# Attention with memory and a bilinear GLU on one core: transfers, roundings and transposed columns set in other places between the matmuls

## The chip, the cores and the metric

One core of a Trainium2 chip runs the whole kernel. The metric is the device time of one execution in microseconds (us), the median of several runs. In the profile the engines are PE (TensorE, matmuls), PEld (its weight loads), DVE (VectorE), ACT (ScalarE), POOL (GpSimd) and SP (SyncE, which mostly issues DMAs).

## What is computed

The input x has 2048 rows of 512. A small vector c gives six modulation vectors (sa, ca, ga, sb, cb, gb). Then, with LN the layernorm of a row:

```python
h = LN(x) * (1 + ca) + sa
x = x + ga * attention(h)        # wq, wk, wv, wo, beta
h = LN(x) * (1 + cb) + sb
x = x + gb * ((h @ w_gate) * (h @ w_up)) @ w_down
```

The attention has 32 heads of 16 columns and goes through 4 segments of 512 rows. In each segment and head it takes a causal softmax, `softmax(q k^T / 4 + mask) v`, and adds to it, with a gate per head, a part from a memory M, z that holds what earlier segments have left (`phi(q) M / (phi(q) z)`). The output of all heads goes through wo. w_gate and w_up have 1376 columns.

## The kernel before

**Numbers.** Where a matmul needs fp32 exactness, each operand is split in a rounded half (H, written by ScalarE as a copy to a rounded format) and a remainder (L, the difference, on VectorE or GpSimd), and three matmuls are done: H with H, H with L, L with H. This is what "roundings" are. Keys and queries are split in three bf16 parts, and laid in DRAM (`kd`, `qd`), from which `load(u)` (L265) brings them as `kst` and `qst`, 384 KB each, for the four heads of a unit.

**Stages.** A prologue makes the modulation vectors, segment 0's layernorm and its first keys, queries and values. Then a loop over v from -2 to 32 handles 32 units u (4 segments x 4 groups of 8 heads x 2 halves) in five slots each. In a slot:

- `q_step`: scores of queries against keys on PE, two banks `q..._0` and `q..._1`, and VectorE's row maxima of them (CUSTOM_DVE q<-q,cmask with READ_ACCUMULATOR nm). The maxima of the unit end in `nm`, which is split and transposed (`n_split`, `n_step`) and written by ScalarE's DMA queue into two rows of qst.
- `k_step`: the transposed scores `k` on PE, one bank; ScalarE's exponential `pt` (L329), GpSimd's causal masking (L332).
- `av_step`: probabilities times values (`tb`), one unit later.
- `t_step`, `r_step`, `o_step`: normalise. The result goes to DRAM (`td`) and back as `rd` and `orow` rows; the reciprocals go to DRAM (`rdd`) and back broadcast as `rb`; VectorE multiplies `orow` by `rb`; the memory's part is added by GpSimd; the row goes to DRAM as `od`. For the last two groups (`last`, ug 14 and 15) PE transposes instead, VectorE divides, and the memory's part is added at L393.

**Filler work.** Between these, `fill(share)` runs pieces of two generators, `fill_a` and `fill_b`, a piece costing as much credit as it yields (0.68 for three matmuls of 512 columns, 0.0 for work off PE). `weave(a, b, at)` puts pieces of b behind those pieces of a whose numbers stand in `at`, counting only pieces that cost credit. So the tables of numbers in these two functions set where each instruction stands in every engine's queue, and each engine works its queue in order.

- `fill_a`: keys, queries and values of the next groups (`a_kq`: 12 matmuls into `kps` or `qps`, from `hH` and `hL`, the split columns of the layernorm), the memory's updates, the next segment's layernorm. Its rows are loaded by `xload` (L580); `ln_rows` takes their statistics on VectorE (BATCH_NORM_STATS2, `ast`) and normalises them; `ln_col` transposes a column block on PE (`atp`), and ScalarE scales it; ScalarE and GpSimd split it (L222, L223).
- `fill_b`: the output projections of segments 0 to 2. `wo_load` (L467) loads `orl` from `od`; `wo_op` (L475) rounds them, `oH` on ScalarE (L497), remainder into `orl` on VectorE; `wo_mm` has four rows of 12 matmuls (`wops`), after each of which VectorE adds to `xr` (`wo_add`) and a DMA writes `x1d` (L535). `lnC` (L542) reads `x1d` back (L548), takes statistics (`cst`), normalises, transposes the columns (`ctp`), scales them (`chf`, L205) and splits them (`chH`, L222): the inputs of the GLU.

After the loop comes the GLU, matmuls `g`, `up` and `acc` closely packed, with no loop work beside them.

**Queues.** SP issues nearly all DMAs in program order; an issue that waits for its data holds up all behind it.

## Time and profile before

| | |
|---|---|
| time, median of 3 runs | 868.21 us (867.92 to 868.63) |
| profiled execution: time | 872.37 us |
| profiled execution: span | 870.6 us |
| mean granted clock of PE | 0.988 |
| PE busy in the span | 833.0 us, 96% |
| DMA, mean rate over the span | 160 GB/s |

A row of a timeline gives start and duration (us), engine, line, operation, output and inputs, and in brackets the idle time ahead of it with what ended it. "x2" is two of them in one row. A row of the list of waits gives the total, the number of times and the longest, all of idle time over a threshold. In the windows, PEclk is the share of full clock that was granted.

### The profile page before, as it was taken

What the parts mean: (1) busy time and instruction counts of PE and PEld (TensorE: products, weight loads), DVE (VectorE), ACT (ScalarE), POOL (GpSimd) and SP (SyncE); (2) the same over time, 40 slices, a digit from 0 to 9 for tenths busy, and PEclk for the clock granted to TensorE, in tenths of its full rate; (3) what the DMA queues carried; (4) which work ended last, traced back from release to release, by engine and by line L of the source; (5) the groups of instructions that cost most, each with busy time, mean ns of one, the idle gap of its engine ahead of it and who ended that gap; (6) DMA issues with size and microseconds to landing.
All of it is one profiled execution on the core that took longest, in us unless ns stands there. A gap on an engine that the chain in (4) does not pass through costs nothing.

```text
span 870.6 us, 14346 instructions
## 1 busy us (share of the span) xinstructions
PE 833.0 (96%) x4824; PEld 584.8 (67%) x4824; DVE 652.7 (75%) x1728; ACT 473.9 (54%) x740; POOL 426.0 (49%) x564
## 2 busy tenths in 40 slices
PE   8999999999999999989988899999999999999998
PEld 5765566566665566655645577788778888887886
DVE  8688677888789777789878769888685666767532
ACT  3747867598667875677445664433354423333321
POOL 4435744487445754496323825998101755650000
PEclk8999999999999999999999999999999999999999
DMA  7773747468566665876794552654305231112033
GB/s 225 224 236 104 220 164 215 147 213 270 181 179 209 220 189 171 247 233 213 234 294 144 171 168 97 181 159 136 108 30 165 70 120 54 50 55 94 0 119 98
DMA packets 111355, 139.45 MB, mean 160 GB/s; under 512 B 18800, under 2 KB 70000, under 8 KB 111280
## 3 DMA queue, kind: packets, MB, share of 16 engines
q1 hardware_dynamic: 106016, 130.91, 49.0%
q10 hardware_dynamic: 5264, 7.62, 2.4%
q8 instruction: 38, 0.62, 0.3%
q14 instruction: 37, 0.30, 0.1%
HBM read 87.48 MB, written 50.76 MB: 159 GB/s over the span
## 4 chain that ended last, share of the span: by engine, by line
PE 70%; DVE 11%; DMA 7%; ACT 7%; issue 2%; POOL 2%; SPq 1%; ACTq 0%; DVEq 0%; POOLq 0%
PE g L90 23%; PE acc L90 14%; PE tb L90 6%; PE k L90 6%; PE q L90 6%; PE vps L90 4%; DVE q L40 4%; PE kps L90 3%; PE qps L90 3%; ACT pt L329 2%; DMA x1d<-xr 2%; PE wops L90 2%; PE up L90 1%; PE mz L90 1%; DVE ast L40 1%
## 5 line engine op out<-in xcount | busy, mean ns | idle before, releaser
L40 DVE CUSTOM_DVE_ANT_0 q<-q,cmask 128x384 f32<-128x384 f32 (+3 forms) x512 | 246.7, 508 | 64.6 <-PE q L90 54.6
L329 ACT ACTIVATE pt<-k 128x1024 f32<-128x1024 f32 x160 | 164.1, 1025 | 65.5 <-PE k L90 51.9
L332 POOL TENSOR_SCALAR_AFFINE_SELECT pt<-pt 128x256 f32<-128x256 f32 (+1 forms) x224 | 107.0, 491 | 148.7 <-ACT pt L329 145.8
L90 PE MATMUL q<-kst,qst 96*128 96x384 bf16 (+3 forms) x512 | 101.5, 302 | 12.1 <-DVE nm L40 9.5
L90 PE MATMUL k<-qst,kst 98*128 98x384 bf16 (+3 forms) x512 | 97.5, 303 | 8.5 <-ACT pt L329 8.4
L448 POOL TENSOR_TENSOR w<-w 128x256 f32<-128x256 f32 (+1 forms) x84 | 72.3, 873 | 57.4 <-DVE t L1216 37.9
L443 POOL TENSOR_TENSOR AL<-w,AH 128x512 fp32r<-128x512 f32 (+1 forms) x42 | 58.8, 1404 | 46.4 <-ACT AH L439 46.3
L90 PE MATMUL tb<-pt,v 128*32 128x512 f32 (+3 forms) x1024 | 78.9, 450 | 1.5 <-POOL pt L332 1.5
L90 PEld LDWEIGHTS <-kst 98*128 98x128 bf16 x512 | 38.5, 99 | 53.9 <-issue 47.5
L40 DVE DVE_READ_ACCUMULATOR2_ANT nm<- 128x1 f32 x512 | 72.4, 141 | 0.0
L439 ACT ACTIVATE AH<-w 128x512 fp32r<-128x512 f32 (+3 forms) x88 | 47.3, 565 | 43.2 <-POOL w L448 29.9
L90 PEld LDWEIGHTS <-qst 96*128 96x128 bf16 x512 | 43.5, 98 | 40.3 <-issue 13.8
L1473 DVE TENSOR_TENSOR mL<-mid,mH 128x512 fp32r<-128x512 f32 (+1 forms) x44 | 32.3, 739 | 41.5 <-ACT mH L1472 41.5
L90 PEld LDWEIGHTS tb<-pt,v 128*32 128x32 f32 x1024 | 29.6, 112 | 41.8 <-issue 36.7
L90 PE MATMUL acc<-DH,mL 128*128 128x512 f32 x144 | 56.6, 393 | 0.9 <-DVE mL L1473 0.9
L90 PE MATMUL acc<-DH,mH 128*128 128x512 f32 x144 | 57.2, 397 | 0.0
L90 PE MATMUL acc<-DL,mH 128*128 128x512 f32 x144 | 56.5, 393 | 0.0
L1472 ACT ACTIVATE mH<-mid 128x512 fp32r<-128x512 f32 (+1 forms) x44 | 27.1, 627 | 51.7 <-PE acc L90 50.4
L1265 ACT ACTIVATE p<-g 128x512 f32<-128x512 f32 (+1 forms) x22 | 13.2, 598 | 74.0 <-PE g L90 73.9
L443 DVE TENSOR_TENSOR AL<-w,AH 128x512 fp32r<-128x512 f32 (+3 forms) x44 | 32.6, 742 | 13.8 <-ACT AH L439 13.6
L358 ACT ACTIVATE tsb<-tb 128x512 f32<-128x512 f32 x32 | 19.1, 597 | 35.2 <-PE tb L90 35.1
L90 PE MATMUL g<-t_0H,AH 128*128 128x512 f32 (+1 forms) x88 | 34.9, 396 | 0.7 <-DVE u L1271 0.3
(286 smaller groups left out, 2067.3 us busy)
## 6 DMA issues: line engine op xcount, KB each, us to landing
kst<-kd SPq DMA_DIRECT2D x32, 384.0 KB
qst<-qd SPq DMA_DIRECT2D x32, 384.0 KB
td<-tsb ACTq DMA_DIRECT2D x28, 256.0 KB
wm<-in_w_mod_dram SPq DMA_DIRECT2D x24, 256.0 KB
kd<-k SPq DMA_DIRECT2D x16, 384.0 KB
qd<-q SPq DMA_DIRECT2D x16, 384.0 KB
w<-in_w_gate_dram SPq DMA_DIRECT2D x20, 256.0 KB
w<-in_w_up_dram SPq DMA_DIRECT2D x40, 128.0 KB
```

The costliest lines, as they stand in the source:

```text
L40: i = getattr(self.eng, name)(*a, **k)
L90: return pe(nc.tensor.matmul(*a, **k))
L329: lpt[0] = act.activation(pt, kp, AF.Exp, scale=0.25)
L332: sels[u, i] = nc.gpsimd.affine_select(w, w, pattern=[[0, w.shape[1]], [1, P]], compare_op=ALU.is_ge, fill=0.0, base=0, channel_multiplier=-1)
L358: act.activation(tsbs[u], tbs.pop(u), AF.Copy)
L439: i = act.activation(hi[sl], w[sl], AF.Copy)
L443: i = eng.tensor_sub(lo[sl], w[sl], hi[sl].bitcast(F32))
L448: i = ce.tensor_tensor(w[:, o, :, 0:n], w[:, x, :, 0:n], w[:, y, :, 0:n], op=op)
L1265: lcp[0] = act.activation(r["p1"], ps, AF.Copy)
L1472: pin(act.activation(mH[0:n], md[0:n], AF.Copy))
L1473: vec.tensor_sub(mL[0:n], md[0:n], mH[0:n].bitcast(F32))
```

## The change

Six things move; the number of matmuls stays.

1. **First rows.** The four rows of segment 1 were loaded two and two: two ahead of the loop's first qst loads, two later behind group 3's weights. Now all four are loaded together, behind the key loads of unit 2 and ahead of group 3's weights. The table STEPS0, which places the steps of their layernorm, follows.
2. **First keys.** For the first group of keys of segments 1 to 3 the matmuls with `hL` are put last.
3. **Last rows' sum.** The addition of L393 goes from GpSimd to VectorE.
4. **Third output's roundings and first output's columns.** `wo_op(2)` and `lnC(0)`'s columns were run one behind the other, after segment 1's output projection; now both are woven between the matmuls of the output projections of segments 1 and 2. `weave` takes several generators for it, and `lnC` has no mark (`yield False`) after each second column any more.
5. **Second output's loads and roundings.** The first two `orl` loads of segment 1 now stand ahead of xr's load, and the roundings begin one piece later.
6. `wo_load` takes the groups to be loaded.

```diff
@@ -226,8 +226,6 @@
             if kept_h is not None:
                 kept_h.append(h)
             yield 0.45
-            if pfx == "c" and d % 2 == 1:
-                yield False
         return hH, hL
 
     def run(gen):
@@ -390,7 +388,7 @@
             vec.reciprocal(rd, tr[:, :, :, DH])
             vec.tensor_mul(orow[:, :, h0:h0 + 4, :], tr[:, :, :, 0:DH], rd.unsqueeze(3).to_broadcast([P, 4, 4, DH]))
             if jq == 1:
-                nc.gpsimd.tensor_add(orows[ug], orows[ug], mems.pop(ug))
+                vec.tensor_add(orows[ug], orows[ug], mems.pop(ug))
             return
         if jq == 0:
             rds[ug] = ap.tile([P, 2, DH], F32, tag="rd", name=f"rd{ug}", bufs=1)
@@ -464,9 +462,9 @@
         wt[i] = hi, lo
         yield 0.0
 
-    def wo_load(s, pool):
+    def wo_load(s, pool, gs=range(NG)):
         rw = []
-        for g in range(NG - 2 if s == NSEG - 1 else NG):
+        for g in gs:
             a = pool.tile([P, L], F32, tag="orl", name=f"orl{s}_{g}", bufs=4)
             pin(nc.sync.dma_start(a, od[s][g]))
             rw.append(a)
@@ -674,16 +672,17 @@
     def a_ln(s):
         return ln(pa, pa, xts.pop(s), s, ca_c, sa_c, "a", ("h", 8, 3), s == 0)
 
-    def weave(a, b, at):
+    def weave(a, *bs):
 
         i = 0
         for w in a:
             yield w
             if w:
-                for _ in range(at.count(i)):
-                    w = next(b, None)
-                    if w or w is False:
-                        yield w
+                for b, at in zip(bs[::2], bs[1::2]):
+                    for _ in range(at.count(i)):
+                        w = next(b, None)
+                        if w or w is False:
+                            yield w
                 i += 1
 
     wH, wL = {}, {}
@@ -763,13 +762,13 @@
         if True:
             dst = kd if nm == "k" else qd
             ps = bank(f"{nm}ps{s}_{g}")
-            n = 0
-            for k in range(KT):
-                for a, b in ((wH, hH), (wL, hH), (wH, hL)):
-                    MM(ps, a[nm, g][:, k, :], b[k], start=n == 0, stop=n == 11)
-                    n += 1
-                    if n in (3, 6, 9):
-                        yield 0.68
+            terms = [(k, a, b) for k in range(KT) for a, b in ((wH, hH), (wL, hH), (wH, hL))]
+            if s > 0 and g == 0 and nm == "k":
+                terms.sort(key=lambda t: t[2] is hL)
+            for n, (k, a, b) in enumerate(terms):
+                MM(ps, a[nm, g][:, k, :], b[k], start=n == 0, stop=n == 11)
+                if n in (2, 5, 8):
+                    yield 0.68
             give()
             f = pa.tile([P, L], F32, tag="f", name=f"{nm}f{s}_{g}", bufs=2)
             fast = s == 0 and g == 0
@@ -971,13 +970,12 @@
     def a_ln_late(s):
         return (yield from a_ln(s))
 
-    STEPS0 = {2: ((3,), (0, 1, 2, 3)), 3: ((1, 1, 2, 2), (0, 1, 2, 3))}
+    STEPS0 = {2: ((1, 3), (0, 1, 2)), 3: ((0, 1, 2, 3), (0, 1, 2, 3))}
     STEPS = {1: ((), (1, 3)), 2: ((0, 1, 2), (1, 3)), 3: ((0, 2), (0, 1, 2, 3))}
 
     def fill_a():
         for w in w2:
             next(w)
-        xts[1] = xload(1, (0, 1))
         yield from av
         memq.extend((a_mem(0, 0), a_mem(0, 1)))
         lns = None
@@ -989,13 +987,14 @@
                     next(mods)
             for g in range(2 if s == 0 else 0, NG):
                 ws = []
+                if s == 0 and g == 2:
+                    xts[1] = xload(1)
                 if s == 0 and g < 3:
                     ws = [load_g(nm, w, g + 1) for nm, w in (("k", wk_), ("q", wq))]
                 for w in ws:
                     next(w)
                 K, Q = a_kq(s, g, "k"), a_kq(s, g, "q")
                 if s == 0 and g == 2:
-                    xts[1] += xload(1, (2, 3))
                     lns = a_ln(1)
                 if 0 < s < 3 and g < 2:
                     K, Q = weave(K, mods, ((), (0, 2))[g]), weave(Q, mods, ((0, 1, 2, 3), ())[g])
@@ -1034,24 +1033,32 @@
     def fill_b():
         open_b()
         pb, bc = B["pb"], B["bc"]
-        rest = wo_mm(0, us[0], xr_load(0, pb, (2, 3)), (2, 3))
-        o1 = wo_load(1, pb)
+        o1 = wo_load(1, pb, (0, 1))
+        xr0 = xr_load(0, pb, (2,))
+        o1 += wo_load(1, pb, (2, 3))
+        rest = wo_mm(0, us[0], xr0 + xr_load(0, pb, (3,)), (2, 3))
         pr = prep(0, "0_0", bc, 1, pb, 1)
         op = wo_op(1, pb, o1, us[1])
-        yield from weave(rest, op, (4, 5, 6, 7))
+        yield from weave(rest, op, (5, 6, 7))
         next(pr)
         B["o0"] = True
-        lg = lnC(0, pb, bc, pb, "x1", 4)
-        yield from weave(wo_mm(1, us[1], xr_load(1, pb)), chain(op, islice(lg, 10)),
-                         (0, 1, 4, 5, 6, 7, 8, 11, 12, 13, 14))
+        lg, o2 = kept_as("nxt", lnC(0, pb, bc, pb, "x1", 4)), third(pb)
+        rest = weave(wo_mm(1, us[1], xr_load(1, pb)), chain(op, lg), (0, 0, 1, 3, 4, 5, 6, 6, 9, 10, 11, 12, 14))
+        yield from weave(rest, o2, (7, 9, 11, 13, 15))
         while "o2" not in B:
             yield None
-        yield from weave(kept_as("nxt", lg), wo_op(2, pb, B["o2"], us[2]), (0, 1, 2, 3, 3))
+        yield from o2
         B["orl_free"] = True
-        lg = lnC(1, pb, bc, pb, "x1", 4)
-        rest = weave(wo_mm(2, us[2], xr_load(2, pb)), lg, (0, 3, 4, 5, 6, 7, 10, 11, 12, 13))
-        yield from weave(rest, pr, (1, 8, 9, 14))
-        B["hf"] = yield from lg
+        lh = lnC(1, pb, bc, pb, "x1", 4)
+        rest = weave(wo_mm(2, us[2], xr_load(2, pb)), lg, (0, 2, 4, 4), lh, (5, 8, 8, 9, 9, 9, 12, 12, 13, 13))
+        yield from weave(rest, pr, (9, 10, 17, 19))
+        B["hf"] = yield from lh
+
+    def third(pb):
+
+        while "o2" not in B:
+            yield 0.0
+        yield from wo_op(2, pb, B["o2"], us[2])
 
     def kept_as(nm, g):
         B[nm] = yield from g
@@ -1146,7 +1153,7 @@
                     av_step(v - 1, kb)
             if v == NQ and slot == 0:
                 assert B["orl_free"]
-                o3 = wo_load(3, B["pb"])
+                o3 = wo_load(3, B["pb"], range(NG - 2))
                 xr3 = xr_load(3, B["pb"])
             if v == NQ and slot == 2:
                 btag[:] = ["ms", "lq0", "ms", "lq1"]
```

Three places of the program, before and after. **Where the loop begins**, SP; `x_0` to `x_3` are segment 1's rows, `kst_224` to `227` and `qst_228` to `231` the four buffers of keys and queries. Before:

```order
L265 DMA kst_225<-kd_0_107 96x2048
L580 DMA x_0_631<-in_x_dram 128x512
L580 DMA x_1_633<-in_x_dram 128x512
L265 DMA qst_228<-qd_0_91 96x2048
L265 DMA qst_229<-qd_0_91 96x2048
L795 DMA kd_1_108<-k_0_1_585 128x512
```

After, from `kst_225` to `kst_227`, with the six issues between `qst_229` and `kst_226` left as they were:

```order
L263 DMA kst_225<-kd_0_107 96x2048
L263 DMA qst_228<-qd_0_91 96x2048
L263 DMA qst_229<-qd_0_91 96x2048
```

```order
L263 DMA kst_226<-kd_1_108 96x2048
L797 DMA qd_1_92<-q_0_1_613 128x512
L578 DMA x_0_682<-in_x_dram 128x512
L578 DMA x_1_684<-in_x_dram 128x512
L578 DMA x_2_686<-in_x_dram 128x512
L578 DMA x_3_688<-in_x_dram 128x512
L263 DMA qst_230<-qd_1_92 96x2048
L706 DMA wrk_690<-in_wk_dram 128x4x128
L706 DMA wrq_694<-in_wq_dram 128x4x128
L263 DMA kst_227<-kd_1_108 96x2048
```

The two x loads ahead of the first qst loads are gone, and all four stand behind `kst_226`, ahead of one qst and of the weights `wrk` and `wrq`.

DVE there, in the maxima of the first two units of segment 0. Before, where the first statistics stand:

```order
L40 ISA q_1_1_761,nm_738<-q_1_1_761,cmask 128x128
L40 ISA nm_738 128x1
L40 BN_STATS ast_0_776<-x_0_631 128x6
L40 BN_AGGR amv_775<-ast_0_776 128x2
L40 ISA q_2_0_796,nm_738<-q_2_0_796,cmask 128x512
L40 ISA nm_738 128x1
L40 ISA q_2_1_799,nm_738<-q_2_1_799,cmask 128x512
L40 ISA nm_738 128x1
L40 BN_STATS ast_1_802<-x_1_633 128x6
L40 BN_AGGR amv_775<-ast_1_802 128x2
```

After, the first statistics of the same rows:

```order
L40 ISA nm_641 128x1
L40 BN_STATS ast_0_716<-x_0_682 128x6
L40 BN_AGGR amv_715<-ast_0_716 128x2
L40 ISA q_4_0_722,nm_641<-q_4_0_722,cmask 128x256
L40 ISA nm_641 128x1
L40 ISA q_4_0_722,nm_641<-q_4_0_722,cmask 128x256
L40 ISA nm_641 128x1
L40 ISA q_4_1_727,nm_641<-q_4_1_727,cmask 128x256
```

Those of row 0 stood in the second unit's maxima (`nm_738`); now they stand in the first unit's (`nm_641`), ahead of its last maxima `q_4`.

**Near the second output's first roundings**, ACT; `pt` are exponentials. Before:

```order
L329 ACTIVATE pt_3_5675<-k_3_5670 128x1024
L497 ACTIVATE oH_0_5714<-orl_0_5628 128x512
L329 ACTIVATE pt_4_5695<-k_4_5690 128x1024
L329 ACTIVATE pt_0_5722<-k_0_5719 128x1024
L497 ACTIVATE oH_1_5776<-orl_1_5630 128x512
L497 ACTIVATE oH_2_5782<-orl_2_5632 128x512
```

After:

```order
L327 ACTIVATE pt_3_5675<-k_3_5670 128x1024
L327 ACTIVATE pt_4_5695<-k_4_5690 128x1024
L327 ACTIVATE pt_0_5720<-k_0_5717 128x1024
L495 ACTIVATE oH_0_5774<-orl_0_5624 128x512
L495 ACTIVATE oH_1_5779<-orl_1_5626 128x512
L356 ACTIVATE tsb_5750<-tb_5733 128x512
```

`oH_0` stood ahead of the exponentials `pt_4` and `pt_0`, and stands behind both now.

**Where the 13th group's rows are normalised and the first output's columns begin**, DVE; `rb` are that group's reciprocals, `x_0_0` to `x_0_3` the rows whose columns are transposed. What "..." leaves out are maxima of `q_2`, `q_3` and `q_4`, and small steps between units. Before, from the multiplication by `rb`:

```order
L40 TENSOR_TENSOR orow_5587<-orow_5587,rb_5949 128x512
...
L40 TENSOR_SCALAR x_0_0_5862<-x_0_0_5862,cmv_5902,cy_6016 128x512
L40 TENSOR_TENSOR xr_2_5826<-xr_2_5826,wops_2_6010 128x512
L40 TENSOR_SCALAR x_0_1_5864<-x_0_1_5864,cmv_5902,cy_6016 128x512
...
L40 TENSOR_SCALAR x_0_2_5866<-x_0_2_5866,cmv_5902,cy_6016 128x512
```

After:

```order
L40 TENSOR_TENSOR orl_0_5854<-orl_0_5854,oH_0_5978 128x512
...
L40 TENSOR_TENSOR orow_5587<-orow_5587,rb_5952 128x512
L40 TENSOR_SCALAR x_0_0_5862<-x_0_0_5862,cmv_5896,cy_5985 128x512
L40 TENSOR_TENSOR orl_1_5856<-orl_1_5856,oH_1_6027 128x512
L40 TENSOR_SCALAR x_0_1_5864<-x_0_1_5864,cmv_5896,cy_5985 128x512
...
L40 TENSOR_SCALAR x_0_2_5866<-x_0_2_5866,cmv_5896,cy_5985 128x512
L40 TENSOR_TENSOR xr_2_5823<-xr_2_5823,wops_2_6023 128x512
L40 TENSOR_TENSOR orl_2_5858<-orl_2_5858,oH_2_6054 128x512
L40 TENSOR_SCALAR x_0_3_5868<-x_0_3_5868,cmv_5896,cy_5985 128x512
```

Three remainders `orl` and the normalisations `x_0_2` and `x_0_3` have come in ahead of this unit's last maxima; `x_0_0` and `x_0_1` stand ahead of `q_3` now.

PE there, the first columns (`ctp`) and the output projections (`wops`). Before:

```order
L90 MATMUL wops_3_6072<-woH_5016,oH_3_5813 128x512
L90 MATMUL wops_3_6072<-woH_5016,orl_3_5634 128x512
L90 MATMUL wops_3_6072<-woL_5083,oH_3_5813 128x512
L93 MATMUL ctp_0_6170<-ident,x_0_0_5862 128x128
L93 MATMUL ctp_0_6170<-ident,x_0_1_5864 128x128
L93 MATMUL ctp_0_6170<-ident,x_0_2_5866 128x128
L93 MATMUL ctp_0_6170<-ident,x_0_3_5868 128x128
L93 MATMUL ctp_1_6183<-ident,x_0_0_5862 128x128
L93 MATMUL ctp_1_6183<-ident,x_0_1_5864 128x128
L93 MATMUL ctp_1_6183<-ident,x_0_2_5866 128x128
L93 MATMUL ctp_1_6183<-ident,x_0_3_5868 128x128
L90 LDWEIGHTS kst_225
```

After:

```order
L93 MATMUL ctp_0_6177<-ident,x_0_0_5862 128x128
L93 MATMUL ctp_0_6177<-ident,x_0_1_5864 128x128
L93 MATMUL ctp_0_6177<-ident,x_0_2_5866 128x128
L93 MATMUL ctp_0_6177<-ident,x_0_3_5868 128x128
L90 MATMUL wops_3_6082<-woH_5016,oH_3_5831 128x512
L90 MATMUL wops_3_6082<-woH_5016,orl_3_5632 128x512
L90 MATMUL wops_3_6082<-woL_5083,oH_3_5831 128x512
L90 MATMUL wops_0_6200<-woH_4890,oH_0_5978 128x512
L90 MATMUL wops_0_6200<-woH_4890,orl_0_5854 128x512
L90 MATMUL wops_0_6200<-woL_4948,oH_0_5978 128x512
L90 LDWEIGHTS kst_225
L90 MATMUL k_3_6204<-qst_229,kst_225 128x384
```

The second column's transposes no longer follow the first's; between stand the last matmuls of `wops_3` and the first of segment 2's `wops_0`.

## The prediction

> **What bounds the kernel now.** I read the page first, then the list of TensorE's waits, then the clock by windows, then the timelines of each engine around the pauses.
>
> ```profile
> span 870.6 us, 14346 instructions
> PE 833.0 (96%) x4824; PEld 584.8 (67%) x4824; DVE 652.7 (75%) x1728; ACT 473.9 (54%) x740; POOL 426.0 (49%) x564
> ```
>
> TensorE (PE) is busy for 833.0 of 870.6 us, and the change leaves its matmuls as they are, only their order differs at four places. So no more than about 37.6 us of idle time is to be had, and besides it the time in which the matmuls run at a lower clock. What an edit is worth is read from the pauses that it touches. The list of TensorE's waits (total us, times, longest) names them:
>
> ```profile
> PE q L90 <- DVE nm L40: 9.5, 19, 1.3
> PE k L90 <- ACT pt L329: 8.4, 13, 2.6
> PE q L90 <- DMA qst<-qd: 2.0, 1, 2.0
> PE tb L90 <- POOL pt L332: 1.5, 1, 1.5
> PE kps L90 <- POOL ahL L223: 0.9, 1, 0.9
> ```
>
> A pause costs more than its length when the clock falls after it. The windows below are cut where the granted clock steps (length, busy us of each engine, PEclk, DMA share, GB/s):
>
> ```profile
> 40.53:43.95 3.42, 1.45 (x7) 1.04 (x7) 0.89 (x3) 0.36 (x1) 2.17 (x2) 1.00 1.03 288
> 43.95:47.37 3.42, 3.42 (x11) 2.19 (x11) 2.23 (x10) 1.10 (x2) 1.16 (x1) 0.50 0.83 292
> 64.44:67.85 3.41, 1.61 (x9) 0.84 (x8) 3.27 (x15) 1.56 (x4) 2.52 (x6) 1.00 0.36 126
> 67.85:71.26 3.41, 3.41 (x17) 1.85 (x15) 2.24 (x10) 1.03 (x1) 0.95 (x4) 0.50 0.10 35
> 436.49:439.90 3.41, 1.67 (x14) 0.77 (x17) 0.90 (x4) 2.52 (x4) 0.63 (x1) 1.00 1.01 320
> 439.90:443.31 3.41, 3.41 (x29) 1.19 (x22) 1.42 (x8) 1.30 (x4) 0.41 (x1) 0.50 0.87 285
> 474.03:477.45 3.42, 1.87 (x12) 1.26 (x11) 2.94 (x11) 1.73 (x3) 0.76 (x2) 1.00 0.03 10
> 477.45:480.87 3.42, 2.17 (x18) 1.58 (x17) 2.34 (x7) 3.42 (x7) 1.44 (x2) 1.00 0.84 229
> ```
>
> In three stretches a window with TensorE busy for 1.45, 1.61 or 1.67 us is followed by one at clock 0.50; one with 1.87 us is followed by full clock. At 0.50, 3.41 us of matmuls do the work of 1.7 us, so each such window costs up to 1.7 us beside the pause that brought it. The Trainium skill, "TensorE: Matmul & The Clock Gate", "Part 1: The HAM clock gate", says that the clock falls to half after a whole idle window of about 3.4 us. This trace differs: no pause listed above is longer than 2.6 us and the clock fell all the same, so the rows decide; by the page none of these pauses would have cost clock, and each term below that holds a half-clock window would be smaller by it.
>
> **First rows** (x loads and their statistics). On SP's queue two x loads stand ahead of the first two qst loads; TensorE's first scores wait for a qst:
>
> ```profile
> 35.53 0.92 SPq L580 DMA_DIRECT2D x<-in_x_dram  x2
> 36.69 0.80 SPq L265 DMA_DIRECT2D qst<-qd  x2
> 47.42 0.43 SPq L707 DMA_DIRECT2D wrk<-in_wk_dram  x1
> ```
> ```profile
> 42.63 0.60 PE L90 MATMUL q<-kst,qst 96*128 96x512 bf16 x2 [1.97 <-DMA qst<-qd]
> ```
>
> Without the x loads the qst loads are issued 36.69 - 35.53 = 1.16 us earlier, and carry no x data ahead of them; the pause is 1.97. So 1.16 to 1.97 us go. The busy time of that window then rises from 1.45 to at least 2.6 us, above the 1.87 that kept full clock, and the half-clock window behind it (1.7 us) goes too: 2.9 to 3.7 in all; I take 3.0, since VectorE (DVE) soon bounds this stretch. Its rows there:
>
> ```profile
> 52.12 0.43 DVE L40 CUSTOM_DVE_ANT_0 q<-q,cmask 128x256 f32<-128x256 f32 x1
> 57.74 0.69 DVE L40 BATCH_NORM_STATS2 ast<-x 128x6 f32<-128x512 f32 x1
> 58.47 0.18 DVE L40 BATCH_NORM_AGGREGATE amv<-ast 128x2 f32<-128x6 f32 x1
> 64.52 0.68 DVE L40 BATCH_NORM_STATS2 ast<-x 128x6 f32<-128x512 f32 x1
> ```
>
> The first statistics (0.69 + 0.18 = 0.87) move ahead of the maxima that start at 52.12, so these come 3.0 - 0.87 = 2.1 us earlier. The statistics at 64.52, ahead of the last maxima of the next unit, move up one place, and with one fewer of them left between the two places, 3.0 us stands from there on. TensorE's longest wait for maxima (1.3) lies in 64.44:67.85; it shrinks by up to 0.87, which brings 1.61 to about 2.5 and saves the half clock at 67.85: 0 to 1.7 us, of which I take 0.6 because VectorE with 3.27 of 3.41 us busy sets much of the pace. First part: 3.0 + 0.6 = 3.6 saved, if the x row has landed when VectorE comes to its statistics. All four x loads now stand where wrk stands above (47.42), and move up with the rest to about 47.42 - 3.0 = 44.4; the weights behind them come later by four issues, some 1.9 us at 0.92 for two, for keys that are two units away. From 36.69 the qst loads took until 42.63, 5.9 us, under full DMA load; by that the row lands at 50.3, VectorE is there at 52.12 - 3.0 = 49.1, and stands for up to 1.2 us. A row of x has less to move than a qst, so I take nothing and keep 0 to 1.2 for the range.
>
> **First keys.** Terms with the rounded-off part of h go last. The wait in question is the 0.9 us for ahL in the list. The last of the four ahL is needed by the same group of matmuls in both orders, and what stands ahead of it only moves the pause: 0, between 0 and -0.9.
>
> **Second output's roundings and its loads, near 435.** The longest wait for ScalarE (ACT), 2.6 us, is here: ACT stands on a rounding whose rows come from HBM, and the exponentials stand behind it.
>
> ```profile
> 436.64 0.63 ACT L497 ACTIVATE oH<-orl 128x512 fp32r<-128x512 f32 x1 [3.50 <-DMA orl<-od]
> ```
>
> The rounding now comes two exponentials later and its loads ahead of an xr load; the 2.6 and the half clock behind (1.7) go, 4.3 us at that place. But the queue of transfers is the next bound. The chain of waits from 423 to 470 runs through DMAs, and VectorE waits at its end:
>
> ```profile
> 429.46 6.44 DMA x1d<-xr
> 437.32 6.65 DMA x1d<-xr
> 448.61 0.63 DVE orl L40
> 458.17 7.60 DMA rb<-rdd
> ```
> ```profile
> 462.62 0.69 DVE L40 BATCH_NORM_STATS2 cst<-x 128x6 f32<-128x512 f32 x1
> 465.86 0.69 DVE L40 TENSOR_TENSOR orow<-orow,rb 128x512 f32<-128x512 f32 x1 [0.44 <-DMA rb<-rdd]
> 468.25 0.54 DVE L40 TENSOR_SCALAR x<-x,cmv,cy 128x512 f32<-128x512 f32 x1
> ```
>
> The DMAs are at their limit near 436 (share 1.01 in the windows), and they carry the same bytes, so rb can land earlier only by what was idle ahead of its issue: between 0 and 4.3 us, and I take 1.0, nearer to nothing since both x1d steps (6.44 and 6.65) remain in the chain. The multiplication at 465.86 stands ahead of the maxima of two groups, so TensorE keeps 1.0 of the 4.3.
>
> **Third output's roundings and first output's columns.** They come earlier by about a unit. Ahead of the maxima that follow 466, VectorE gets three remainders (orl, 0.63 in the row at 448.61, say 0.65) and two normalisations (0.54), and loses one statistic (0.87): 1.95 + 1.08 - 0.87 = 2.2 us later; a normalisation fewer later gives back 0.5. With a pause so lengthened the clock may fall once more: 0 to 1.7, I take 0.8. So the region 423 to 473 comes to -1.0 + 2.2 - 0.5 + 0.8 = +1.5. Then the pauses where ACT had carried roundings, columns and exponentials together:
>
> ```profile
> 476.50 0.33 PE L93 MATMUL ctp<-ident,x 128*128 128x128 f32 x1 [1.28 <-DVE x L40]
> 477.09 0.66 PE L93 MATMUL ctp<-ident,x 128*128 128x128 f32 x4 [0.27 <-DVE xr L40]
> 480.31 0.60 PE L90 MATMUL k<-qst,kst 98*128 98x256 bf16 x4 [1.25 <-ACT pt L329]
> 482.78 0.59 PE L90 MATMUL k<-qst,kst 98*128 98x512 bf16 x2 [0.56 <-ACT pt L329]
> ```
>
> 1.28 + 0.27 + 1.25 + 0.56 = 3.4 us. The roundings are off ACT by then and the columns are spread one by one, with matmuls of the output projection between; a new wait for the first column copy (the column's ACT pass queues behind an exponential) takes back about 0.5: -2.9, bounds 0 and -3.4.
>
> **Last rows' sum.** TensorE's 1.5 us wait for POOL lies behind this addition:
>
> ```profile
> 495.99 1.74 POOL L393 TENSOR_TENSOR orow<-orow,memb 128x512 f32<-128x512 f32 x1
> ```
>
> On VectorE it costs about 0.69 (as the multiplication at 465.86), where VectorE has work of no haste; POOL's mask comes 1.74 earlier. I take -1.2, bounds 0 and -1.5. Near 514 the second such sum runs beside VectorE:
>
> ```profile
> 514.70 1.67 DVE L40 TENSOR_TENSOR t<-chf,t 128x512 f32<-128x512 f32 x1
> 516.29 0.68 DVE L40 TENSOR_TENSOR t<-chf,chf 128x512 f32<-128x512 f32 x1
> ```
>
> Moved to VectorE it adds 0.69 and, if the stretch of 1.67 against 0.68 comes from it, takes 0.99 away: 0, bounds -0.3 and +0.7.
>
> **The sum**: -3.6 + 0 + 1.5 - 2.9 - 1.2 + 0 = -6.2 us. The profiled execution had a span of 870.6 us and took 872.37, 4.2 above the median of 868.21; its pauses are taken to be those of any execution, so the span becomes 864.4, and the median 868.21 - 6.2 = 862.0. Differences under 0.2% (1.7 us) can't be told from no change.
>
> **Rivals.**
> - The transfers near 435 move up with TensorE: nothing waits at 465.86, the 4.3 us are kept and no half clock is lost. That is 3.3 + 0.8 better than the sum: -10.3, 857.9. For it: rb's issue at 458.17 stands behind work that TensorE and VectorE release. Against it: the DMA share of 1.01. Chance 0.20.
> - The x row lands just so late that the first part brings nothing (about 52.7): -2.6, 865.6. Chance 0.15.
> - Slower: the x row lands much later, and VectorE, which works strictly in order, stands at its statistics with the maxima of all heads behind it. The longest load of such a row that I see is the one that ended in the statistics at 462.62:
>
> ```profile
> 454.76 1.07 SPq L548 DMA_DIRECT2D x<-x1d  x1
> ```
>
> 7.9 us. If the loads are issued as late as wrk before, 47.42, that gives 55.3. The maxima would then start at 55.3 + 0.87 = 56.2 instead of 52.12, +4.1; less 0.87 later, +3.2; and a half-clock window after so long a pause, 1.7: +4.9 in place of -3.6, so +2.3 in all, 870.5. It decides from a landing at 54.8 on (+1.7 in all). Against it: the DMA share falls to 0.83 in the window of the issue. The Trainium skill, "DMA: Bandwidth & Descriptors", "Two DMAs through the same engine are not ordered", says that nothing orders transfers across the 16 engines, so the place in the queue promises no landing; that no run here shows by itself. Chance 0.13.
> - The change moves the time nowhere, because VectorE sets the pace in the first part and transfers set it in the later one: 868.2. Chance 0.02.
>
> **Numbers.** The forecast has 0.50, with a range of its own from 859 to 865 (first part 1.2 less; the region at 435 1.5 to either side; the pauses at 476 to 483 a third less). 857.0 to 868.5 takes in all but the slower rival and the ends. Faster by over 0.2% (under 866.5): forecast and first rival 0.70 and two thirds of the second, 0.80. Within 0.2%: the rest of the second, the last, and a part of the third's lower end, 0.08. Slower: 0.12.
>
> **What would show it.** Right: no 2 us pause and full clock between 40 and 47; VectorE at the first statistics of segment 1 by 50 without a wait for x; no 3.5 us idle of ACT near 436, and rb still waited for near 464; pauses between 475 and 483 under 1 us together; no 1.5 us wait for POOL near 498. Wrong: VectorE idle at the first statistics with x as the releaser, a new half-clock window near 55 or 466, or longer waits of TensorE for nm near 470 than the 2.2 us above.

## The result and the profile after

The changed kernel took 873.93 us (median of 6 runs, 871.35 to 876.07), the kernel before 867.76 us beside it (6 runs, 866.93 to 868.63): a ratio of 1.0067, interval 1.0047 to 1.0086. It is slower by 6.2 us, where 6.2 us less was forecast. Its profiled execution took 874.40 us, with a span of 872.6. The engines' busy time in it:

```profile
PE 832.4 (95%) x4824; PEld 585.0 (67%) x4824; DVE 651.6 (75%) x1730; ACT 474.6 (54%) x740; POOL 422.1 (48%) x562
```

The busy times are those of before; what differs is who waits. TensorE's waits after:

```profile
PE q L90 <- DVE nm L40: 13.8, 22, 2.6
PE k L90 <- ACT pt L327: 5.3, 13, 0.9
PE tb L90 <- POOL pt L330: 2.6, 1, 2.6
PE wops L90 <- DVE orl L40: 1.7, 1, 1.7
PE q L90 <- DMA qst<-qd: 0.4, 1, 0.4
```

What the prediction wanted gone has gone: ScalarE's 8.4 is 5.3 and its longest 0.9, the wait for qst is 0.4. But VectorE's 9.5 has become 13.8, GpSimd's 1.5 has become 2.6, and 1.7 for a remainder `orl` is new. The three longest pauses each fill most of a clock window (length, busy us of PE, PEld, DVE, ACT, POOL, then PEclk, DMA share, GB/s):

```profile
52.19:55.60 3.41, 1.44 (x10) 1.13 (x9) 3.24 (x15) 0.00 (x0) 0.00 (x0) 1.00 0.90 238
55.60:59.01 3.41, 3.41 (x13) 2.32 (x12) 3.08 (x13) 0.52 (x1) 0.00 (x0) 0.50 1.11 244
465.19:468.60 3.41, 0.63 (x4) 0.19 (x2) 3.34 (x9) 1.02 (x1) 2.14 (x3) 1.00 0.00 0
468.60:472.01 3.41, 3.06 (x18) 0.90 (x21) 3.38 (x11) 0.00 (x0) 0.00 (x0) 0.50 0.27 94
495.91:499.32 3.41, 1.19 (x20) 0.52 (x16) 3.01 (x8) 0.40 (x1) 3.41 (x4) 1.00 0.20 77
499.32:502.73 3.41, 3.06 (x13) 1.67 (x14) 0.00 (x0) 1.57 (x3) 0.85 (x3) 0.50 0.20 77
```

Behind TensorE's windows of 1.44, 0.63 and 1.19 us follows half the clock, as the prediction read it before, and at 445 it follows a window of 1.72; only the places are others: near 55, 445, 469 and 500. The Trainium skill ("TensorE: Matmul & The Clock Gate", "Part 1: The HAM clock gate") asks for a whole idle window; here the clock fell behind windows with up to 1.72 us of work, so the rows decide.

Where the time comes and goes is seen by following one matmul through the traces. Each number is the start of the same matmul in a kernel's trace less its start in the trace of `keys` (an experiment below, whose span, 866.2 us, is the nearest to the usual one), less the same difference at 428 us; so it tells what was lost since 428. The first column is apart: lost from the first scores (41 us) to 86 us.

```
                41-86 |  438   446   461   470   487   502   519
keys              0.0 |  0.0   0.0   0.0   0.0   0.0   0.0   0.0
before           +0.6 | +0.2  +0.2  -0.9  -1.0  -1.0  -1.0  -0.9
after            +1.5 | -3.3  -0.7  -0.8  +3.4  -0.3  +3.0  +3.7
first            +1.8 | -2.0  -1.7  -1.7  -1.3  +0.2  +0.2  +0.2
sum              -0.7 | -2.4  -2.4  -1.0  -1.2  +0.3  -0.7  -0.4
late             -1.4 | -3.5  -2.4  -1.7  +3.9  +0.2  +5.7  +6.3
cols             -0.7 | -3.4  -0.8  -1.9  -0.1  -1.4  +2.8  +3.6
round            -1.4 | -3.6  -0.6  -0.6  -0.2  +1.8  +1.8  +1.8
loads            -1.4 | -3.5  -0.5  -1.1  -0.4  +1.5  +1.5  +1.5
col3             -1.4 | -3.6  -2.5  -2.1  +3.8  +0.1  +0.8  +1.6
col3_sum         -1.4 | -3.7  -2.6  -3.4  +3.7  +0.1  -0.1  +6.2
after_col3       +1.9 | -3.7  -2.7  -2.5  +3.5  -0.2  -0.3  +5.4
after_gp_col3    +1.3 | -3.9  -2.8  -2.3  +3.2  -0.4  +0.2  +1.0
after_round      +3.0 | -3.5  -0.5  -0.6  +0.4  +1.5  +0.7  +0.7
after_cols       +0.3 | -3.8  -2.6  -2.4  +4.0  +1.4  +1.3  +7.8
cols_col3        -1.4 | -3.6  -2.5  -3.6  +3.4  +3.0  +3.6  +4.5
loads4           -1.4 | -3.6  -3.6  -1.6  -1.6  -1.6  -1.6  -1.6
pool             -1.4 | -0.4  -0.4  -1.2  -0.6  -0.6  -0.6  +0.5
```

The row of `after` is a curve of gains and losses: -3.3 at 438 (ScalarE's pause near 435 and the half clock behind it, which `keys` has too), +2.6 by 446 (a remainder, with half the clock behind it), +4.2 by 470 (VectorE), -3.7 by 487 (the columns' pauses), +3.3 by 502 (GpSimd's mask). One execution is behind each row, and a half-clock window more or less is 1.7 us.

### The profile page after: what moved, and what is told of

Same layout as the page of the kernel before. It is cut to its first block, busy times and chain, and to the rows that moved or that the text cites. A ratio compares the mean times of both kernels' runs of the same rounds, so it can differ in the third digit from the quotient of the medians.

```text
span 872.6 us, 14353 instructions
## 1 busy us (share of the span) xinstructions
PE 832.4 (95%) x4824; PEld 585.0 (67%) x4824; DVE 651.6 (75%) x1730; ACT 474.6 (54%) x740; POOL 422.1 (48%) x562
## 4 chain that ended last, share of the span: by engine, by line
PE 71%; DMA 7%; ACT 6%; DVE 6%; POOL 5%; issue 3%; SPq 1%; ACTq 0%; POOLq 0%; DVEq 0%
PE g L90 23%; PE acc L90 14%; PE tb L90 6%; PE k L90 5%; PE q L90 5%; PE vps L90 4%; PE kps L90 3%; PE qps L90 3%; PE wops L90 3%; DVE q L40 2%; ACT pt L327 2%; DMA x1d<-xr 1%; DMA orow<-td 1%; PE up L90 1%; PE mz L90 1%
## 5 line engine op out<-in xcount | busy, mean ns | idle before, releaser
L330 POOL TENSOR_SCALAR_AFFINE_SELECT pt<-pt 128x256 f32<-128x256 f32 (+1 forms) x224 | 104.1, 479 | 151.5 <-ACT pt L327 146.8
L90 PE MATMUL q<-kst,qst 96*128 96x384 bf16 (+3 forms) x512 | 101.5, 301 | 14.6 <-DVE nm L40 13.8
L1479 ACT ACTIVATE mH<-mid 128x512 fp32r<-128x512 f32 (+1 forms) x44 | 27.1, 627 | 51.7 <-PE acc L90 50.4
L90 PE MATMUL g<-chH,AH 128*128 128x512 f32 (+1 forms) x88 | 34.8, 395 | 0.7 <-ACT p L1272 0.7
```

Of the source, the lines that this page charges most:

```text
L90: return pe(nc.tensor.matmul(*a, **k))
L330: sels[u, i] = nc.gpsimd.affine_select(w, w, pattern=[[0, w.shape[1]], [1, P]], compare_op=ALU.is_ge, fill=0.0, base=0, channel_multiplier=-1)
L1479: pin(act.activation(mH[0:n], md[0:n], AF.Copy))
```

## The experiments

The letters in the expectations are theories, in the order in which they came up.

**Which part.** Four kernels each make one separable part of the change alone. `first` is part 1:

```diff
-    STEPS0 = {2: ((3,), (0, 1, 2, 3)), 3: ((1, 1, 2, 2), (0, 1, 2, 3))}
+    STEPS0 = {2: ((1, 3), (0, 1, 2)), 3: ((0, 1, 2, 3), (0, 1, 2, 3))}
...
-        xts[1] = xload(1, (0, 1))
...
+                if s == 0 and g == 2:
+                    xts[1] = xload(1)
...
-                    xts[1] += xload(1, (2, 3))
```

> Only the first part of the change (all four x loads of segment 1 together, later, and the table of steps that follows). Theory A (the late edits in fill_b cost the time): this part is worth little, since in the traces TensorE stands at +0.85 us against before ahead of the first scores (38 us) and at +0.17 at 80 us; expected -1 to +1 us against before. Theory B (the x row lands late, VectorE stands 1.6 us, TensorE 2.6 us, and the clock falls): +3 to +5 us, most of the change's loss.

870.09 us, 1.0010 (0.9989 to 1.0031): no gain of 3.6, and no loss that can be told from none. `keys` is part 2:

```diff
...
+            if s > 0 and g == 0 and nm == "k":
+                terms.sort(key=lambda t: t[2] is hL)
...
```

> Only the first keys' order of terms. All theories: within 1 us of before, and in the trace the wait for ScalarE's half takes over what the wait for GpSimd's half loses (0.94 us before, near 91).

868.07 us, 1.0002 (0.9979 to 1.0026). `sum` is part 3:

```diff
-                nc.gpsimd.tensor_add(orows[ug], orows[ug], mems.pop(ug))
+                vec.tensor_add(orows[ug], orows[ug], mems.pop(ug))
```

> Only the last rows' sum on VectorE. Theory A and B alike: -1.5 to 0 us, by the 1.5 us wait of TensorE for GpSimd near 498 that stands behind this addition. Rival: it is the cause of the loss near 510, then +1 to +2.

869.82 us, 1.0002 (0.9977 to 1.0027). TensorE's wait for the last mask shrank as forecast, in its trace from 1.47 to 0.39:

```profile
496.90 0.64 PE L90 MATMUL tb<-pt,v 128*32 128x256 f32 x8 [0.39 <-POOL pt L332]
```

and the time did not follow. `late` is parts 4 to 6 (`weave`, `wo_load`, `third`, all of `fill_b`, no `yield False`), whose core is

```diff
-        yield from weave(rest, op, (4, 5, 6, 7))
+        yield from weave(rest, op, (5, 6, 7))
...
+        yield from weave(rest, o2, (7, 9, 11, 13, 15))
...
+        rest = weave(wo_mm(2, us[2], xr_load(2, pb)), lg, (0, 2, 4, 4), lh, (5, 8, 8, 9, 9, 9, 12, 12, 13, 13))
```

> Only the late edits: fill_b with its loads, the roundings of the third output and the columns of the first output woven between the projections, no marks between columns. Theory A: +3 to +6 us, most of the change's loss; the trace of the changed kernel goes from -2.5 us at 430 to +2.2 us at 510 against before. Theory B: within 1.5 us of before.

875.18 us, 1.0074 (1.0042 to 1.0105): the late parts alone carry the whole loss.

**Which of the late parts.** `cols` is `late` with the third roundings in one piece, so that only the columns are woven; `round` is `late` with the columns as before, so that only the roundings are; `loads` is the kernel before with part 5 alone.

```diff
-        yield from weave(rest, o2, (7, 9, 11, 13, 15))
+        yield from rest
```

> The late edits, but with the third output's roundings in one piece ahead of its projection, as before, and only the first output's columns woven. Theory C (the three remainders ahead of the maxima near 465 cost TensorE about 4 us there, the first of them stretched from 0.69 to 1.75 us beside GpSimd's sum): the wait of 3.8 us near 463 falls under 2 us, and the time is 3 to 4 us below that of the late edits (about 871.5). Theory D (GpSimd's queue in the last units, near 495, makes the loss): the time stays within 1.5 us of the late edits (about 875).

875.48 us, 1.0067 (1.0043 to 1.0091).

```diff
-        rest = weave(wo_mm(1, us[1], xr_load(1, pb)), chain(op, lg), (0, 0, 1, 3, 4, 5, 6, 6, 9, 10, 11, 12, 14))
+        rest = weave(wo_mm(1, us[1], xr_load(1, pb)), chain(op, islice(lg, 10)),
+                     (0, 1, 4, 5, 6, 7, 8, 11, 12, 13, 14))
...
+        yield from kept_as("nxt", lg)
...
```

> The late edits, but with the first output's columns as before (one behind the other, after the roundings), and only the third output's roundings woven. Theory C: still 2 us or more over before, with a wait for maxima near 463 of over 2.5 us. Theory D: the waits for GpSimd near 495 fall from 3.2 us to about 1.5 us as before and the time is 3 us or more below that of the late edits.

871.30 us, 1.0019 (0.9993 to 1.0046).

```diff
-        o1 = wo_load(1, pb)
+        o1 = wo_load(1, pb, (0, 1))
+        xr0 = xr_load(0, pb, (2,))
+        o1 += wo_load(1, pb, (2, 3))
...
-        yield from weave(rest, op, (4, 5, 6, 7))
+        yield from weave(rest, op, (5, 6, 7))
```

> Of the late edits only the order of the second output's loads and its roundings one piece later. Theory of the record (the 4.3 us at 435 are given back, since the broadcast of the reciprocals lands no earlier): the wait of 2.0 to 2.6 us near 435 is gone, VectorE waits 2 us or more for that broadcast near 460, and the time is within 1 us of before. Rival (transfers move up too): 3 to 4 us below before.

870.97 us, 1.0010 (0.9982 to 1.0037). So the woven columns carry most of it, and the theory that blamed the remainders ahead of the maxima near 465 (C) falls as the account of the whole loss: it expected 3 to 4 us less of `cols`, which has them away from there, and `cols` is as slow. From 461 to 470 the trace of `cols` loses 1.8 us where that of `late` loses 5.6, but one execution doesn't settle this place. `cols_col3`, an experiment below with the same instructions up to there, loses 7.0, because `rb` came late:

```profile
463.43 0.69 DVE L40 TENSOR_TENSOR orow<-orow,rb 128x512 f32<-128x512 f32 x1 [3.25 <-DMA rb<-rdd]
```
```profile
466.95 0.58 PE L90 MATMUL q<-kst,qst 96*128 96x256 bf16 x2 [3.79 <-DVE nm L40]
```

VectorE's wait for `rb` and TensorE's for the maxima behind it are 0.59 and 1.39 in `cols`, 1.57 and 3.81 in `late`. So TensorE waits some 1.5 us longer than `rb` accounts for where the remainders stand there, and the rest hangs on `rb`. In `late` more time goes at GpSimd, later. Its queue and TensorE's wait:

```profile
487.77 2.57 POOL L446 TENSOR_TENSOR w<-w 128x256 f32<-128x256 f32 x3
...
491.55 1.73 POOL L391 TENSOR_TENSOR orow<-orow,memb 128x512 f32<-128x512 f32 x1
...
495.88 1.26 POOL L223 TENSOR_TENSOR chL<-chf,chH 128x512 fp32r<-128x512 f32 x1
497.10 0.99 POOL L330 TENSOR_SCALAR_AFFINE_SELECT pt<-pt 128x512 f32<-128x512 f32 x2
```
```profile
494.05 1.07 PE L90 MATMUL tb<-pt,v 128*32 128x384 f32 x16 [0.50 <-POOL pt L330]
497.79 1.08 PE L90 MATMUL tb<-pt,v 128*32 128x256 f32 x8 [2.67 <-POOL pt L330]
```

The fourth column's remainder `chL` (1.26) now stands right ahead of the last masks; before, the last of them ended at 489.3, nine us ahead of that mask:

```profile
484.12 1.17 POOL L448 TENSOR_TENSOR w<-w 128x256 f32<-128x256 f32 x1
...
486.08 0.74 POOL L448 TENSOR_TENSOR w<-w 128x256 f32<-128x256 f32 x1
486.77 2.54 POOL L223 TENSOR_TENSOR chL<-chf,chH 128x512 fp32r<-128x512 f32 x2
489.26 1.29 POOL L443 TENSOR_TENSOR AL<-w,AH 128x512 fp32r<-128x512 f32 x1
...
498.89 0.64 POOL L332 TENSOR_SCALAR_AFFINE_SELECT pt<-pt 128x512 f32<-128x512 f32 x1
```

`col3` tests this (theory D): `late` with the fourth column's remainder on VectorE (of all outputs; in the kernels below, of the first output alone).

```diff
-                nc.gpsimd.tensor_sub(lo, h, hi.bitcast(F32))
+                (vec if pfx == "c" and d == 3 else nc.gpsimd).tensor_sub(lo, h, hi.bitcast(F32))
```

> The late edits, with the remainder of the first output's fourth column (1.26 us on GpSimd ahead of the last masks) taken on VectorE. Theory D: the wait for the last mask near 495 falls from 2.67 to about 1.4 us, and the time is 1.5 to 3 us below that of the late edits, the clock's fall after it included. Theory C: within 1 us of the late edits.

871.05 us, 1.0022 (0.9993 to 1.0050): 4 us back. The wait is shorter,

```profile
496.42 0.64 PE L90 MATMUL tb<-pt,v 128*32 128x256 f32 x8 [1.44 <-POOL pt L330]
```

and from 487 to 502 it loses 0.7 where `late` lost 5.5: 1.2 of pause, and the two half-clock windows that `late` has behind it (497.1 to 503.9) and `col3` has not.

**The same cure in the whole change, and GpSimd's load by itself.** `after_col3` is the whole change with col3's edit, `after_cols` with all four remainders of the first output on VectorE, `loads4` is `loads` with one rounding left a piece earlier, and `pool` is the kernel before with the memory's part of the 15th group added twice on GpSimd (so its output holds that part twice).

```diff
+                (vec if pfx == "c" and s == 0 and d == 3 else nc.gpsimd).tensor_sub(lo, h, hi.bitcast(F32))
```

> The whole change, with the remainder of the first output's fourth column on VectorE instead of GpSimd. Theory D (GpSimd's queue ahead of the last masks near 497, with the half clock that follows, is most of the loss): 868.5 to 871.5, 3 to 5 us below the change as it stands (873.9); the wait for the last mask falls from 2.6 to about 1.3 us. If the loss of the whole change lies elsewhere (x row, maxima at 465): within 1.5 us of 873.9.

878.44 us, 1.0101 (1.0050 to 1.0151).

```diff
+                (vec if pfx == "c" and s == 0 else nc.gpsimd).tensor_sub(lo, h, hi.bitcast(F32))
```

> The whole change, with the remainders of all four columns of the first output on VectorE. Theory D: GpSimd has 5 us less to do ahead of the last masks, so the wait near 497 is gone and the time is at or below before: 866 to 869. If VectorE takes the place of GpSimd as the bound there: 870 to 873, with new waits for maxima or remainders between 478 and 500.

877.36 us, 1.0101 (1.0067 to 1.0135), where 866 to 869 was expected, or 870 to 873 with VectorE as the new bound.

```diff
-        yield from weave(rest, op, (5, 6, 7))
+        yield from weave(rest, op, (4, 5, 6, 7))
```

> Before with the new order of the second output's loads alone; the roundings stand where they stood. Theory E (the 1.69 us wait for a remainder near 440 in the kernel with loads and later roundings comes from the roundings' later place): that wait is gone, the wait near 435 for the exponential is under 1 us since the rows have landed earlier, and the time is 1 to 3 us below before. Rival (the rows land no earlier): ScalarE stands on the rounding as before, wait of 2 us or more, time within 1 us of before.

869.39 us, 1.0018 (0.9989 to 1.0047).

```diff
+                if ug == NSEG * NG - 2:
+                    nc.gpsimd.tensor_add(orows[ug], orows[ug], mems[ug])
```

> Before, with the memory's part of the 15th group added twice on GpSimd, near 497, so that output differs; it doubles one suspected cost, 1.3 to 1.7 us of GpSimd ahead of the last masks. Theory D: TensorE's wait for the mask grows from 1.5 to about 3 us, and the time by 1.5 us plus one or two falls of the clock (1.7 us each) in part of the executions: +2 to +5 us. If the masks have slack there: under +0.5 us.

868.92 us, 1.0000 (0.9976 to 1.0024). `pool` tells nothing: the doubled sum came to stand behind the last mask, not ahead of it.

```profile
494.32 0.63 POOL L332 TENSOR_SCALAR_AFFINE_SELECT pt<-pt 128x512 f32<-128x512 f32 x1
...
496.54 1.29 POOL L395 TENSOR_TENSOR orow<-orow,memb 128x512 f32<-128x512 f32 x1
```

In `loads` TensorE waits 1.69 us for a remainder at 443.9, as in the changed kernel (its row stands further below). `loads4` is without that wait and, in its trace, 3.1 us ahead of `loads` at 519, yet its median can be told neither from `loads`'s nor from before's. `after_col3` and `after_cols` brought nothing back (1.0101 each, with intervals that overlap that of the changed kernel), although their rows in the table show the cure at work: nothing is lost from 487 to 502. `after_col3` loses 5.8 later, where VectorE stands for the second output's `cy`, the factor of its normalisation, which ScalarE works out in two small steps and GpSimd in five:

```profile
508.32 1.43 DVE L40 TENSOR_SCALAR x<-x,cmv,cy 128x512 f32<-128x512 f32 x2 [4.51 <-POOL cy L191]
```
```profile
503.34 0.19 POOL L188 TENSOR_SCALAR cyb<-cmv 128x4 f32<-128x4 f32 x1
...
505.40 1.29 POOL L441 TENSOR_TENSOR AL<-w,AH 128x512 fp32r<-128x512 f32 x1
506.65 0.20 POOL L187 TENSOR_TENSOR cya<-cy 128x4 f32<-128x4 f32 x1
...
508.09 0.20 POOL L191 TENSOR_TENSOR cy<-cy,cyb 128x4 f32<-128x4 f32 x1
```

Between the statistics (end 503.1) and `cy` (508.3) lie 5.2 us, of which GpSimd's five steps, of 0.19 to 0.20 each, are 1; they stand behind masks and an `AL` of 1.29. In `col3` the statistics end at 497.4 and `cy` is there at 500.2, 2.8 us.

**Why the cure fails there.** Theory F: the last rows' sum, on VectorE by part 3, stands ahead of these statistics and puts the chain behind others' work. It is tested from both sides: `col3_sum` is `col3` with part 3 added (and, unlike `col3`, with the remainder moved for the first output alone), `after_gp_col3` is `after_col3` with part 3 taken back. `cols_col3` joins `cols` and col3's edit, `after_round` is the whole change without the woven columns.

```diff
-                nc.gpsimd.tensor_add(orows[ug], orows[ug], mems.pop(ug))
+                vec.tensor_add(orows[ug], orows[ug], mems.pop(ug))
```

> The late edits with the fourth column's remainder on VectorE, and the last rows' sum on VectorE as in the whole change. Theory F (the sum on VectorE puts off the second output's statistics, so its scale comes late through GpSimd's queue and TensorE waits at its columns): 4 us or more over the same kernel with the sum on GpSimd, so about 875 to 878, with a wait of 3 us in all for normalised rows near 508. If the first rows or first keys took the gain in the whole change: about 871.

874.61 us, 1.0073 (1.0044 to 1.0102), against 1.0022 without the sum.

```diff
-                vec.tensor_add(orows[ug], orows[ug], mems.pop(ug))
+                nc.gpsimd.tensor_add(orows[ug], orows[ug], mems.pop(ug))
```

> The whole change with the last rows' sum left on GpSimd and the fourth column's remainder on VectorE. Theory F: 869 to 872, no wait for normalised rows over 1 us near 508. If the first rows or first keys took the gain: 875 to 878.

871.47 us, 1.0043 (1.0027 to 1.0059), against 1.0101 with it. F holds: the intervals of each pair touch only at their ends, both pairs go the same way, and the traces agree. From 502 to 519 the three kernels with the sum on VectorE and the last masks in time lose 6.2 (`col3_sum`), 5.8 (`after_col3`) and 6.5 us (`after_cols`), the three without it 0.8 each (`col3`, `after_gp_col3`, `cols_col3`). The sum puts the end of the statistics 0.9 us later (498.3 in `col3_sum`, 497.4 in `col3`), and `cy` comes 3.3 us later (503.5 and 500.2). Of TensorE's waits there, `col3_sum` has four:

```profile
504.12 0.33 PE L93 MATMUL ctp<-ident,x 128*128 128x128 f32 x1 [1.21 <-DVE x L40]
505.01 0.44 PE L93 MATMUL ctp<-ident,x 128*128 128x128 f32 x1 [0.56 <-DVE x L40]
506.08 0.93 PE L93 MATMUL ctp<-ident,x 128*128 128x128 f32 x2 [0.64 <-DVE x L40]
507.47 1.11 PE L93 MATMUL ctp<-ident,x 128*128 128x128 f32 x4 [0.45 <-DVE xr L40]
```

2.9 us of pauses, and the clock falls to half behind them (505 to 512).

```diff
-        yield from weave(rest, o2, (7, 9, 11, 13, 15))
+        yield from rest
...
+                (vec if pfx == "c" and s == 0 and d == 3 else nc.gpsimd).tensor_sub(lo, h, hi.bitcast(F32))
```

> The late edits with the roundings in one piece and the columns woven, with the fourth column's remainder on VectorE. Theory D, limited to the late edits without the sum on VectorE: 870 to 872, 4 us below the same kernel with that remainder on GpSimd (875.5). If the gain of that remainder was peculiar to the kernel it was seen in: 874 or more.

872.97 us, 1.0051 (1.0030 to 1.0071): between the two answers that were expected, and its interval overlaps that of `cols` (1.0043 to 1.0091), so the time settles nothing. Its trace loses 0.6 from 487 to 502 where that of `cols` loses 4.2, but has the 3.25 us for `rb` ahead of it.

```diff
-        rest = weave(wo_mm(1, us[1], xr_load(1, pb)), chain(op, lg), (0, 0, 1, 3, 4, 5, 6, 6, 9, 10, 11, 12, 14))
+        rest = weave(wo_mm(1, us[1], xr_load(1, pb)), chain(op, islice(lg, 10)),
+                     (0, 1, 4, 5, 6, 7, 8, 11, 12, 13, 14))
...
+        yield from kept_as("nxt", lg)
...
```

> The whole change without the woven columns: the first output's columns come one behind the other as before, all else as changed. If the woven columns carry the loss also here: 868 to 871, within 0.3% of before. If other parts of the whole change carry it: 873 or more.

871.47 us, 1.0034 (1.0012 to 1.0055): without the woven columns half of the loss stays. Its parts (`first` 1.0010, `loads` 1.0010, `round` 1.0019, which holds `loads`) can't be told from none one by one, so how that half divides stays open. `after_gp_col3`, which has both cures, still takes 1.0043, and its interval overlaps that of the changed kernel; its trace loses 5.5 us from 461 to 470, and no experiment takes that place by itself in the whole change. No version here is faster than the kernel before.

## Why the prediction was wrong

**The profiled execution was taken as the usual one.** The prediction noted that it took 4.2 us more than the median, and went on with "its pauses are taken to be those of any execution". That step failed for the terms in which a half-clock window was to go (1.7 near 44, 0.6 near 68, and 1.7 in the 4.3 near 435). Eleven other traces, those without part 1, hold the very same instructions up to 70 us. None of them has the window at 44, three have the one near 68 (`keys`, `sum`, `cols`), and their pause for qst is 0.69 to 2.01, in the mean 1.24 and not 1.97. Of four others with the same instructions near 435, two have the half clock there (`keys`, `pool`) and two have not (`first`, `sum`). The 120 executions of the kernel before beside the experiments have a mean clock of 0.9930 and spans from 863.1 to 875.6; over them a span grows by 0.61 us for each us of clock lost (a straight line through all of them). The profiled one had 0.988. So of the first part's 3.6 the 1.7 near 44 was clock that none of the other executions had lost, and the 0.6 near 68 was lost in some of them. The six executions of the changed kernel average 0.9885, 3.9 us of clock more lost than before; by the same slope that is 2.4 us of the 6.2.

**First rows, -3.6.** It was worth nothing: 1.0010 alone. The x loads were issued late, at 46.93 instead of the 44.4 that was reckoned, behind a `qd` write at 46.51 that stands ahead of them in SP's order. Before, this write was issued at 46.99, so it moved up by 0.5 and not by the 3.0 of the sum:

```profile
46.93 1.91 SPq L578 DMA_DIRECT2D x<-in_x_dram  x4
```
```profile
51.76 0.69 DVE L40 BATCH_NORM_STATS2 ast<-x 128x6 f32<-128x512 f32 x1 [1.61 <-DMA x<-in_x_dram]
```
```profile
53.63 0.38 PE L90 MATMUL q<-kst,qst 96*128 96x512 bf16 x1 [2.61 <-DVE nm L40]
```

The row landed at 51.7, 4.8 us behind the issue; VectorE stood 1.61, TensorE 2.61, and half the clock followed. That is the mechanism of the slower rival, at 51.7 rather than its 54.8. (The 7.9 us from which that rival was reckoned is an upper bound: no wait stands ahead of the statistics at 462.62.) It is not there in each execution: of six kernels with part 1, `after` (1.61) and `after_round` (2.12) show the wait for x, four don't, and in those too TensorE waits 0.9 to 1.1 for the maxima behind the statistics, where `keys` waits 0.16. Against that stands the gain at qst, where the six wait 0.43 to 1.10, in the mean 0.68: some 0.6 us, not 1.2 to 2.0. So the gain at qst is given back at the maxima even where the row is in time.

**First keys, 0.** Right: the pause only moves, from the remainder's 0.94 to the rounded half's 1.19, and 0.24 for the remainder is left.

```profile
90.66 0.51 PE L90 MATMUL kps<-ahH,wkH 128*128 128x512 f32 x1 [1.19 <-ACT ahH L222]
92.33 0.50 PE L90 MATMUL kps<-ahL,wkH 128*128 128x512 f32 x1 [0.24 <-POOL ahL L223]
```

**Near 435.** The pause is gone as forecast and `rb` is still waited for (0.36, below), so most of the gain was to be given back by 466. In the whole change it was given back sooner: the roundings that begin one piece later make their remainders one piece later, and TensorE stands for one at 443. The prediction costed that move at nothing.

```profile
443.35 0.50 PE L90 MATMUL wops<-woH,orl 128*128 128x512 f32 x1 [1.69 <-DVE orl L40]
```

**Woven roundings and columns, +2.2 near 466.** The direction was right, the size was not: from 428 to 470 the change's trace loses 4.4 us against that of before (+3.4 and -1.0 in the table), where +1.5 was booked. VectorE, from the multiplication by `rb` to the maxima, and GpSimd beside it:

```profile
463.46 0.69 DVE L40 TENSOR_TENSOR orow<-orow,rb 128x512 f32<-128x512 f32 x1 [0.36 <-DMA rb<-rdd]
464.07 0.54 DVE L40 TENSOR_SCALAR x<-x,cmv,cy 128x512 f32<-128x512 f32 x1
464.53 1.76 DVE L40 TENSOR_TENSOR orl<-orl,oH 128x512 fp32r<-128x512 f32 x1
466.21 0.85 DVE L40 TENSOR_SCALAR x<-x,cmv,cy 128x512 f32<-128x512 f32 x1
```
```profile
464.24 1.50 POOL L416 TENSOR_TENSOR orow<-orow,memb 128x512 f32<-128x512 f32 x1 [1.68 <-DVE orow L40]
```
```profile
468.04 0.38 PE L90 MATMUL q<-kst,qst 96*128 96x256 bf16 x2 [2.60 <-DVE nm L40]
```

The remainder was put at 0.65 and took 1.76 beside GpSimd's sum, the second normalisation 0.85 instead of 0.54: 1.4 us more, just ahead of the maxima. The pause of 2.60 empties the clock's window to 0.63 us, and the half clock came in full instead of the 0.8 that was booked. From 461 to 470 the change loses 4.2 us. In all seven traces with both woven parts TensorE's pause here is VectorE's wait for `rb` and 2.1 to 2.3 us more (`rb` 0.36 to 2.42, pause 2.60 to 4.58); with the columns alone woven it is `rb` and 0.8 (`cols`) or 0.5 (`cols_col3`). So the landing of `rb`, from which the sum kept 1.0 us, decides much of what is lost here, and it differs widely between executions.

**Pauses from 475 to 483, -2.9.** Right: TensorE is busy for 7.83 of 8 us there, where it had been 4.64:

```profile
475.00:483.00 8.00, 4.64 (x35) 3.25 (x33) 6.40 (x23) 6.43 (x11) 3.94 (x6) 1.00 0.38 103
```
```profile
475.00:483.00 8.00, 7.83 (x53) 5.51 (x52) 7.03 (x26) 6.31 (x9) 4.33 (x8) 1.00 0.52 168
```

The only pause left is 0.17, and 3.7 us come back by 487. What was not asked is what is late next.

**Last rows' sum, -1.2 near 497.** With the first rows this is the term furthest off: 1.2 us were to be gained, and from 487 to 502 the change loses 3.3. The sum did leave GpSimd's queue, and alone it shortened the wait (0.39). But in the changed kernel more came into this queue than left it: a column's remainder, two of the four `w` steps (they stood at 484 to 487 before) and an `AL` (at 489.26 before):

```profile
490.45 2.57 POOL L446 TENSOR_TENSOR w<-w 128x256 f32<-128x256 f32 x3
492.99 1.72 POOL L441 TENSOR_TENSOR AL<-w,AH 128x512 fp32r<-128x512 f32 x1
...
496.54 1.27 POOL L223 TENSOR_TENSOR chL<-chf,chH 128x512 fp32r<-128x512 f32 x1
497.77 1.27 POOL L416 TENSOR_TENSOR orow<-orow,memb 128x512 f32<-128x512 f32 x1
498.98 1.00 POOL L330 TENSOR_SCALAR_AFFINE_SELECT pt<-pt 128x512 f32<-128x512 f32 x2
```
```profile
499.68 1.08 PE L90 MATMUL tb<-pt,v 128*32 128x256 f32 x8 [2.57 <-POOL pt L330]
```

2.57 us instead of 0.3, and half the clock from 499.3. The prediction read GpSimd's queue at this place only for the one instruction that left it, not for those that would come in. It also named VectorE's work there "of no haste"; the statistics of the second output are in that queue, and `col3_sum` shows what the sum ahead of them costs (some 4 us) once the masks are in time. In the changed kernel itself that second price is hidden by the first; `after_col3` uncovers it.

So of four forecast gains only the one from 475 to 483 came in full. Of the rivals, the two about the x row named what happened in the first part; none named GpSimd's queue near 497, where `col3` got back 4 of the late parts' 6.5 us.

## What to carry to other kernels

A pause that goes is a gain only as far as it is there in the usual execution, so compare the profiled one's clock and time with the median before its half-clock windows are booked. When work is woven between other work, go through every in-order queue that it enters (here GpSimd's ahead of the causal masks) and ask what stands behind it, not only through the one that it leaves. A chain of tiny steps over three engines (statistics, square root, `cy`) costs what stands ahead of each step in its queue, and so a sum of 1 us (1.04 in `col3_sum`) ahead of its start could cost 4 us at its end.
